# Adding x on GpSimd in SBUF, in place of an identity product on TensorE, for eight output row blocks of a fused attention and gMLP kernel

## The chip, the cores and the metric

One core of a Trainium2 chip runs the kernel. The metric is the device time of one execution in microseconds (us). The kernel before took 169.01 us as the median of three runs (168.78 to 170.12). The execution that was profiled took 168.79 us, of which 167.0 us are the span of the profile. Differences under 1% are not told from no change here.

## The reference

Windowed attention with four sink tokens feeds a gMLP block with spatial gating. All inputs are f32; B = 4, H = 8, S = 768, D = 64, the model width H·D is 512, and d_ff is 1024.

```python
# attention
keep = is_sink | in_window                  # sink: pos < 4; window: 0 <= rel < 128
scores = np.where(keep, q @ k.T / sqrt(D), -1e9)
a = softmax(scores)
x = (a @ v), heads side by side             # (B, S, 512)
# gMLP
h = gelu_tanh(x @ w_in)                     # (B, S, 1024)
u, v = h[..., :512], h[..., 512:]
v_n = (v - mean(v)) / sqrt(var(v) + 1e-6) * g_ln
v_s = einsum('ts,bsd->btd', w_sg, v_n) + b_sg[None, :, None]
out = x + (u * v_s) @ w_out
```

The last line is what the change touches: the sum of the projection and x.

## The kernel before

A batch element is called a block here; there are four, numbered 0 to 3 in the code and first to last in the text. Each has four head pairs, so 16 pairs `n` run through the attention: casts to bf16 on GpSimd (L104, L107), transposes, scores on TensorE (`sc`, L264), exponentials on ScalarE (`ex`, L277), masks on VectorE (L286) or GpSimd (L294, L296), products with v on TensorE (`av`, L320, L326), and the division on VectorE (L328, L329), which leaves x in SBUF as bf16 (`x_sb`, three buffers, one for each block in work).

With the four pairs of a block done, `hidden` runs its first gMLP part: products with w_in (`hv`, `hu`), Gelu on ScalarE, statistics (`st`, L372), an inverse root by nine small VectorE steps (L393 to L402), and six normalising steps (`vn`, L408). The second part of a block is cut into units that wait in a list, `fillers`: eight spatial units (six products `vs`, L418, and then on VectorE `gv`, L421, and `gT`, L424), and six projections, one for each 128 output rows (`project`, a group of four products `o_ps`, L449). The code takes units from that list with `fill` while the attention of the next block runs; so a block's projections stand among the attention of the block behind it. For the blocks before the last the rows are projected in the order 0, 2, 4, 1, 3, 5. The last two or three of a block (rows 3 and 5 of the second, rows 1, 3 and 5 of the third) are taken at the end of the next block's `hidden`, beside its vn steps. The last block has no attention behind it: its units run at the end, with rows 0, 1 and 2 in between the spatial units and rows 3, 4 and 5 at the close; row 5 is cut in two halves (`project_last`).

x reaches the output in one of two ways. With `by_act` false, VectorE adds x while it takes the sum out of PSUM (L452). With `by_act` true, TensorE adds it as a fifth product with an identity matrix (L455), and ScalarE copies the bank to SBUF (L458). Either way SyncE issues the store (L459). The odd rows of the blocks before the last, and all but row 3 of the last, go by ScalarE.

The order on each engine is the order of the program text (`manual_schedule`); nothing moves an instruction. Four PSUM banks turn in `ps_m`, and six SBUF tiles `o_sb` hold rows on their way out. A check at the end counts good reciprocals (L469 to L480, loaded by every engine at L753) and branches to a general version that does not run here.

Of the kernel before, what the change touches and what calls it, by code (L numbers as in the profile page):

```python
# [18 lines left out]
def kernel(  # L19
# [14 lines left out]
    nc = tc.nc  # L34
    V, G, A = nc.vector, nc.gpsimd, nc.scalar
# [7 lines left out]
    NT = S // 128  # L43
    HP = H // 2
    KD = DM // 128
    KU = DF // 128
    NP = B * HP
    HT = NT // 2
# [52 lines left out]
    def cast(n, which, eng):  # L101
        src = raw.pop((n, which))
        if which == "v":
            eng.tensor_copy(v_bufs[n % NV][:, :, :, 0:64], src)  # L104
            return
        dst = work.tile([128, NT, 128], BF16, name=which + "_bf")
        eng.tensor_copy(dst.rearrange("p t (h d) -> p h t d", h=2), src)  # L107
        flat[n, which] = dst

    def load_all(n):  # L110

        for which, m in (("k", n), ("q", n), ("v", n - 1)):
            if m < NP:
                load(m, which, in_rows=m >= FIRST)

    def cast_all(n, parts="kqv"):
        for which in parts:
            m = n - 1 if which == "v" else n
            if m < NP:
                cast(m, which, G)  # L120
# [27 lines left out]
    for i in range(WARM):  # L148
# [3 lines left out]
        out=halves[:, :, 0, :], in_=halves[:, :, 0, :], compare_op=ALU.is_ge, fill=DARK,  # L152
        base=0, pattern=[[0, 2], [1, 128]], channel_multiplier=-1)
    G.affine_select(
        out=halves[:, :, 1, :], in_=halves[:, :, 1, :], compare_op=ALU.is_ge, fill=DARK,
# [53 lines left out]
    def bank(shape, dtype, name):  # L209
        return ps_m.tile(shape, dtype, name=name, tag="m")  # L210

    kTs, qTs, exps, avs = {}, {}, {}, {}
    x_sb, xT = {}, {}
# [85 lines left out]
    def begin_x(b):  # L299
        x_sb[b] = work.tile([128, HP, NT, 128], BF16, name="x", bufs=3)  # L300
        xT[b] = work.tile([128, HP, S], BF16, name="xT")
# [139 lines left out]
                A.copy(o_sb, o_ps[:, 0:m])  # L441
            (nc.sync if eng is V else A).dma_start(out=out[b, rows, cols], in_=o_sb)

    def project(b, t, by_act):
        rows = slice(128 * t, 128 * (t + 1))
        o_ps = bank([128, 512], F32, "o_ps")
        o_sb = small.tile([128, DM], F32, name="o_sb", bufs=6)
        for c in range(KU):
            nc.tensor.matmul(o_ps, gTs[b][:, c, rows], w_out_sb[:, c, :],  # L449
                             start=(c == 0), stop=(c == KU - 1 and not by_act))  # L450
        if not by_act:
            V.tensor_add(o_sb.rearrange("p (h d) -> p h d", h=HP),  # L452
                         o_ps.rearrange("p (h d) -> p h d", h=HP), x_sb[b][:, :, t, :])
        else:
            nc.tensor.matmul(o_ps.rearrange("p (h d) -> p h d", h=HP), iden, x_sb[b][:, :, t, :],  # L455
                             start=False, stop=True)
        if by_act:
            A.copy(o_sb, o_ps)  # L458
        nc.sync.dma_start(out=out[b, rows, :], in_=o_sb)  # L459


    LEAST, MOST = 1e-20, 1e20
# [20 lines left out]
    def general():  # L483
        W = 256 + n_sink
        wide = work.tile([128, 3, W], F32, name="wide", tag="ex", bufs=3)
        V.memset(wide, 1.0)
        m = [wide[:, i, :] for i in range(3)]
        for i in range(3):
            G.affine_select(out=m[i][:, 0:128], in_=m[i][:, 0:128], compare_op=ALU.is_gt,
                            fill=0.0, base=0, pattern=[[1, 128]], channel_multiplier=-1)  # L490
            G.affine_select(out=m[i][:, 128:256], in_=m[i][:, 128:256], compare_op=ALU.is_ge,
                            fill=0.0, base=0, pattern=[[-1, 128]], channel_multiplier=1)
        V.memset(m[0][:, 0:128], 0.0)
        V.memset(m[0][:, 128:128 + n_sink], 0.0)
        V.memset(m[1][:, 0:n_sink], 0.0)
        low = work.tile([128, 3, W], F32, name="low", tag="ex", bufs=3)
        V.tensor_scalar(out=low, in0=wide, scalar1=-1.0, scalar2=1e9,
                        op0=ALU.add, op1=ALU.mult)
        for b in range(B):
            begin_x(b)  # L500
            for hp in range(HP):
                n = HP * b + hp
                for which in "kqv":
                    load(n, which)
                for which in "kqv":
                    cast(n, which, V)
                columns(n, "k", A)
                columns(n, "q", V)
                for i in range(NT):
                    for l in range(2):  # L510
                        stable(n, i, l, m[min(i, 2)], low[:, min(i, 2), :])
                turn_x(n, V)
            hidden(b, {})
            fill(len(fillers))

    def stable(n, i, l, keep, low):
        b, hp = divmod(n, HP)
# [36 lines left out]


    fillers = []

    def fill(count=1):
        for _ in range(count):
            if fillers:  # L560
                fillers.pop(0)()

    def hidden(b, between):
        units = [lambda j=j: hidden_v(b, j) for j in range(NT)]
        units += [lambda f=f, n=n: hidden_u(b, f, n) for n in range(2) for f in range(KU)]
        after = {NT + 1: [lambda: inverse_root(b)]}
        for j in range(NT):
            after.setdefault(NT + 1 + j, []).append(lambda j=j: normalise(b, j))
        for i, unit in enumerate(units):
            unit()  # L570
            for step in after.get(i, []) + between.get(i, []):
                step()
        gate = [[lambda f=f, n=n: spatial(b, f, n) for f in range(KU)] for n in range(2)]
        if b < B - 1:
            fillers.extend(gate[0] + gate[1])
            fillers.extend(lambda t=t: project(b, t, t % 2 == 1) for t in (0, 2, 4, 1, 3, 5))
            return

        rows = [lambda t=t: project(b, t, t != HT) for t in range(NT - 1)]
        fillers.extend(gate[0] + [gate[1][0], rows[0], gate[1][1], gate[1][2], rows[1],  # L580
                                  gate[1][3]] + rows[2:])
        fillers.append(lambda: project_last(b, NT - 1))
# [94 lines left out]
    LAST = NT + 2 * KU - 1  # L677
# [6 lines left out]
    for n in range(HP, NP):  # L684
        todo = valued < n - 1
        block = n % HP == 0 and n > HP
        if HP < n <= 2 * HP:
            load_all(n + 3)
        if n not in exps:
            score(n, 0, 1)  # L690
        if n == HP:
            for si in range(3, NT):
                turn_weights(si, V)
        keep_band(n, 0, V)
        keep_band(n, 1, G)
        if n + 2 >= FIRST:
            cast_all(n + 2, "kq")
        if todo:
            values(n - 1, 0)
        fill(2 if n > HP and not todo else 1)  # L700
        if n + 1 < FIRST and not block:
            columns(n + 1, "k", A)
        if n == HP:
            columns(n + 1, "q", V)
            fill()
        score(n, 2)
        keep_band(n, 2, G)
        if todo:
            values(n - 1, 1)
            if x_by_dma(n - 1):  # L710
                turn_x_by_dma(n - 1)
        if FIRST <= n + 2 < NP:
            columns_by_dma(n + 2)
            if n + 4 == FIRST + 2:
                load_all(n + 4)
        if QUOTA[n] > 2 and todo:
            fill()
        if HP < n < FIRST - 1 and not block:
            columns(n + 1, "q", A if todo else V)
        if n + 2 <= NP:  # L720
            cast_all(n + 2, "v" if n + 2 >= FIRST else "kqv")
        if QUOTA[n] > 1:
            fill()
        if block:
            open_v(n // HP - 1, 0)
            open_v(n // HP - 1, 1)
        if todo and not x_by_dma(n - 1):
            turn_x(n - 1, V)
        if block:
            open_v(n // HP - 1, 2)  # L730
        valued = n - 1
        if block:
            hidden(n // HP - 1, {1: [lambda: values(n, 0)], 3: [lambda: values(n, 1)],
                                 5: [lambda: columns(n + 1, "k", A)] if n + 1 < FIRST else [],
                                 6: [lambda m=m: load_all(m) for m in later.get(n, ())],
                                 7: [lambda: columns(n + 1, "q", A)] if n + 1 < FIRST else [],
                                 9: [lambda: turn_x_by_dma(n) if x_by_dma(n) else turn_x(n, V)],
                                 LAST: [lambda: score(n + 1, 0, 1), lambda: fill(2)]})
            valued = n
# [7 lines left out]
    open_v(B - 1, 2)  # L747
    seen = {}
    hidden(B - 1, {2: [lambda: seen.update(c=count_good())],
                   LAST: [lambda: fill(3)]})  # L750
    seen["t"] = total(seen["c"])
    fill(4)
    count = nc.values_load(seen["t"][0:1, 0:1], min_val=0, max_val=128 * NP * NT * 2)  # L753
# [39 lines left out]
```

## Time and profile before

| | |
|---|---|
| median of three runs | 169.01 us |
| profiled execution | 168.79 us |
| its span | 167.0 us |
| mean granted TensorE clock | 0.993 |
| PE busy | 155.6 us (93%), 1558 matmuls |
| DVE busy | 131.8 us (79%) |
| ACT busy | 109.1 us (65%) |
| POOL busy | 78.1 us (47%) |
| identity products for x, L455 | 13, 379 ns each |
| copies of o_ps by ScalarE, L458 | 13, 593 ns each |
| additions by VectorE, L452 | 10, 682 ns each |
| stores of o_sb, L459 | 23, 256 KB each, median 2.3 us to landing |

PE is TensorE, PEld its weight loads, DVE VectorE, ACT ScalarE, POOL GpSimd, SP SyncE. Matmuls are pipelined, so the 379 ns of one are not its price: consecutive identity or projection products start about 0.22 us apart. The shares of busy time are averages over stages with different limits, so the prediction goes by the stage that each edit stands in.

### The profile page before, as it was taken

What the parts mean: (1) busy time and instruction counts of PE and PEld (TensorE: products, weight loads), DVE (VectorE), ACT (ScalarE), POOL (GpSimd) and SP (SyncE); (2) the same over time, 40 slices, a digit from 0 to 9 for tenths busy, and PEclk for the clock granted to TensorE, in tenths of its full rate; (3) what the DMA queues carried; (4) which work ended last, traced back from release to release, by engine and by line L of the source; (5) the groups of instructions that cost most, each with busy time, mean ns of one, the idle gap of its engine ahead of it and who ended that gap; (6) DMA issues with size and microseconds to landing.
All of it is one profiled execution on the core that took longest, in us unless ns stands there. A gap on an engine that the chain in (4) does not pass through costs nothing.

```text
span 167.0 us, 4051 instructions
## 1 busy us (share of the span) xinstructions
PE 155.6 (93%) x1558; PEld 91.1 (55%) x1558; DVE 131.8 (79%) x317; ACT 109.1 (65%) x148; POOL 78.1 (47%) x115
## 2 busy tenths in 40 slices
PE   3979999999999999999999999999999989999960
PEld 3535574666567665565665655554565635545530
DVE  6756874996899986799888994989999939887620
ACT  3198878889977689688887367679754068621130
POOL 6479771105899979400289996001985000000000
PEclk9999999999999999999999999999999999999997
DMA  4999979999999979999903999899931310050343
GB/s 140 329 323 263 205 104 282 213 317 287 283 220 296 279 247 351 295 215 224 205 20 67 132 238 210 190 228 216 177 76 34 130 63 0 0 194 2 122 151 122
DMA packets 60194, 31.09 MB, mean 186 GB/s; under 512 B 48356, under 2 KB 57080, under 8 KB 60168
## 3 DMA queue, kind: packets, MB, share of 16 engines
q1 hardware_dynamic: 56800, 27.47, 68.8%
q0 software_dynamic: 2944, 2.77, 10.3%
q10 hardware_dynamic: 424, 0.53, 0.9%
q8 instruction: 14, 0.23, 0.6%
q14 instruction: 12, 0.10, 0.2%
HBM read 24.81 MB, written 6.29 MB: 186 GB/s over the span
## 4 chain that ended last, share of the span: by engine, by line
PE 70%; DVE 17%; DMA 5%; issue 1%; ACT 1%; SPq 1%; POOL 1%; POOLq 0%; ACTq 0%
PE vs L418 13%; PE o_ps L449 10%; PE hu L380 9%; PE hv L361 8%; PE av L320 7%; PE sc L264 6%; DMA k_sb<-in_k_dram 5%; DVE gT L424 3%; DVE gv L421 3%; PE hv L368 3%; PE xps L337 2%; DVE st L372 2%; PE av L326 2%; PE qps L219 2%; PE kps L219 2%; DVE vn L408 2%
## 5 line engine op out<-in xcount | busy, mean ns | idle before, releaser
L277 ACT ACTIVATE ex<-sc 128x1024 bf16<-128x1024 f32 x48 | 47.5, 1024 | 12.7 <-PE sc L264 9.2
L418 PE MATMUL vs<-wsgT,vn 128*128 128x384 bf16 x192 | 35.5, 326 | 0.1
L294 POOL TENSOR_SCALAR_AFFINE_SELECT ex<-ex 128x512 bf16<-128x512 bf16 x25 | 17.0, 680 | 30.7 <-issue 15.2
L418 PEld LDWEIGHTS <-vn 128*128 128x128 bf16 x192 | 17.7, 98 | 10.7 <-DVE tot L480 0.4
L449 PE MATMUL o_ps<-w_out_sb,gT 128*128 128x512 bf16 x92 | 23.5, 379 | 0.0
L380 PE MATMUL hu<-xT,w_in_sb 128*128 128x384 bf16 x128 | 22.1, 326 | 0.0
L421 DVE SCALAR_TENSOR_TENSOR gv<-vs,g_sb,b_bc 128x384 bf16<-128x384 f32 x32 | 19.6, 612 | 3.1 <-PE vs L418 2.7
L372 DVE BATCH_NORM_STATS2 st<-v_all 128x6 f32<-128x512 f32 x24 | 16.1, 671 | 5.8 <-ACT v_all L370 5.8
L361 PE MATMUL hv<-w_in_sb,xT 128*128 128x512 bf16 x72 | 18.8, 379 | 0.7 <-ACT v_all L370 0.7
L107 POOL CAST k_bf<-k_sb 128x768 bf16<-128x768 f32 x15 | 13.1, 870 | 13.0 <-DMA k_sb<-in_k_dram 9.0
L329 DVE TENSOR_TENSOR x<-av,rcps 128x384 bf16<-128x384 f32 x32 | 17.8, 557 | 1.1
L424 DVE TENSOR_TENSOR gT<-gv,uT 128x384 bf16<-128x384 bf16 x32 | 17.0, 532 | 1.9
L383 ACT ACTIVATE uT<-hu 128x384 bf16<-128x384 f32 x32 | 15.7, 493 | 4.1 <-PE hu L380 3.7
L458 ACT COPY o_sb<-o_ps 128x512 f32<-128x512 f32 x13 | 7.4, 593 | 14.3 <-PE o_ps L455 12.8
L264 PE MATMUL sc<-qT,kT 64*128 64x256 bf16 x192 | 15.7, 264 | 1.1 <-DVE qT L225 0.7
L380 PEld LDWEIGHTS <-w_in_sb 128*128 128x128 bf16 x128 | 12.3, 98 | 8.0
L370 ACT ACTIVATE v_all<-hv 128x512 f32<-128x512 f32 x24 | 13.1, 600 | 5.0 <-PE hv L368 4.6
L320 PE MATMUL av<-v_sb,ex 128*128 128x65 bf16 x352 | 16.1, 194 | 0.0
L104 POOL CAST v_sb<-v_sb 128x768 bf16<-128x768 f32 x16 | 14.5, 909 | 2.4 <-DMA v_sb<-in_v_dram 2.4
L320 PEld LDWEIGHTS <-ex 128*128 128x128 bf16 x352 | 13.1, 98 | 4.3 <-issue 1.1
L107 POOL CAST q_bf<-q_sb 128x768 bf16<-128x768 f32 x15 | 13.9, 925 | 2.9 <-DMA q_sb<-in_q_dram 2.9
L296 POOL TENSOR_SCALAR_AFFINE_SELECT ex<-ex 128x512 bf16<-128x512 bf16 (+1 forms) x25 | 14.4, 574 | 0.0
(88 smaller groups left out, 218.0 us busy)
## 6 DMA issues: line engine op xcount, KB each, us to landing
k_sb<-in_k_dram SPq DMA_DIRECT2D x16, 384.0 KB, 6.0
v_sb<-in_v_dram SPq DMA_DIRECT2D x16, 384.0 KB, 6.3
out_dram<-o_sb SPq DMA_DIRECT2D x23, 256.0 KB, 2.3
q_sb<-in_q_dram SPq DMA_DIRECT2D x15, 384.0 KB, 5.7
wsg_sb<-in_moe_w_sg_dram POOLq DMA_DIRECT2D x2, 576.0 KB, 10.9
w_in_sb<-in_moe_w_in_dram POOLq DMA_DIRECT2D x2, 256.0 KB, 6.4
w_in_sb<-in_moe_w_in_dram POOLq DMA_DIRECT2D x1, 512.0 KB, 5.4
w_out_sb<-in_moe_w_out_dram POOLq DMA_DIRECT2D x1, 512.0 KB, 9.3
```

What stands on the lines that cost most here:

```text
L107: eng.tensor_copy(dst.rearrange("p t (h d) -> p h t d", h=2), src)
L264: nc.tensor.matmul(sc[:, 512 * l + w:512 * l + w + n_q], kT[rows, 128 * j:128 * (j + 1)], qT[rows, 128 * j:128 * j + n_q], start=not dark, ...
L277: A.activation(out=exps[n][:, g, :], in_=sc, func=AF.Exp, scale=scale)
L320: nc.tensor.matmul(av[:, m, l, :], probs(j, l, half), v_sb[:, l, j, :], start=first, stop=False)
L329: V.tensor_mul(x_sb[b][:, hp, HT * c:HT * (c + 1), :].rearrange("p i (l d) -> p i l d", l=2), av[:, :, :, 0:64], rcp.to_broadcast([128, HT ...
L361: nc.tensor.matmul(hvs[b, j], xT[b][:, c, 128 * j:128 * (j + 1)], w_in_sb[:, c, DF:], start=(c == 0), stop=False)
L372: V.bn_stats(out=st, in_=v_alls[b][:, j, :])
L380: nc.tensor.matmul(h_ps[:, 0:NH], w_in_sb[:, c, 128 * f:128 * (f + 1)], xT[b][:, c, NH * n:NH * (n + 1)], start=(c == 0), stop=(c == KD - 1))
L418: nc.tensor.matmul(vs[:, 0:NH], vns[b][:, si, 128 * f:128 * (f + 1)], wsgT[:, si, cols], start=(si == 0), stop=(si == NT - 1))
L421: V.scalar_tensor_tensor(out=gv, in0=vs[:, 0:NH], scalar=g_sb[:, f:f + 1], in1=b_bc[:, cols], op0=ALU.mult, op1=ALU.add)
L424: V.tensor_mul(gTs[b][:, f, cols], gv, uTs[b][:, f, cols])
L449: nc.tensor.matmul(o_ps, gTs[b][:, c, rows], w_out_sb[:, c, :], start=(c == 0), stop=(c == KU - 1 and not by_act))
```

## The change

Eight of the 13 rows that ScalarE takes out of PSUM lose their identity product: rows 3 and 5 of the second block, rows 1, 3 and 5 of the third, and rows 0, 1 and 2 of the last. For these ScalarE copies the plain sum to `o_sb`, GpSimd adds x to it in place, and then the store is issued. Additions and stores are put off: `project` notes the row in a list, and `add_late` works it off at three places, in the loop over pairs behind the casts, at the end of the last block's `hidden` behind the three projections there, and behind each row of the last block. In GpSimd's queue the second block's two additions come behind the cast of v that follows the masks of pair 13, ahead of the masks of pair 14; the third block's three come before the load of the check's count, the last block's three behind it.

```diff
-    def project(b, t, by_act):
+    late = []
+
+    def project(b, t, by_act, by_pool=False):
...
-                             start=(c == 0), stop=(c == KU - 1 and not by_act))
+                             start=(c == 0), stop=(c == KU - 1 and (by_pool or not by_act)))
+        if by_pool:
+            A.copy(o_sb, o_ps)
+            late.append((b, t, o_sb))
+            return
...
+    def add_late():
+
+        while late:
+            b, t, o_sb = late.pop(0)
+            o = o_sb.rearrange("p (h d) -> p h d", h=HP)
+            G.tensor_add(o, o, x_sb[b][:, :, t, :])
+            nc.sync.dma_start(out=out[b, 128 * t:128 * (t + 1), :], in_=o_sb)
...
+    held = {0: (), 1: (3, 5), 2: (1, 3, 5)}
...
-            fillers.extend(lambda t=t: project(b, t, t % 2 == 1) for t in (0, 2, 4, 1, 3, 5))
+            fillers.extend(lambda t=t: project(b, t, t % 2 == 1, t in held[b]) for t in (0, 2, 4, 1, 3, 5))
...
-        rows = [lambda t=t: project(b, t, t != HT) for t in range(NT - 1)]
+        def row(t):
+            project(b, t, t != HT, t < HT)
+            add_late()
+
+        rows = [lambda t=t: row(t) for t in range(NT - 1)]
...
@@ loop over pairs @@
             cast_all(n + 2, "v" if n + 2 >= FIRST else "kqv")
+        add_late()
...
-                   LAST: [lambda: fill(3)]})
+                   LAST: [lambda: fill(3), add_late]})
```

More of the change, by code (lines that the diff above doesn't have):

```diff
@@ L721 @@
             cast_all(n + 2, "v" if n + 2 >= FIRST else "kqv")
+        add_late()
         if QUOTA[n] > 1:
```

## The prediction

> **What bounds the kernel now.** The chain of waits on the page comes first: shares of the span by engine.
>
> ```profile
> PE 70%; DVE 17%; DMA 5%; issue 1%; ACT 1%; SPq 1%; POOL 1%; POOLq 0%; ACTq 0%
> ```
>
> TensorE carries 70% of the path, so one instruction fewer there seems to pay. But it need not pay where the eight instructions stand, so the chain in order of time is read next, from 110 us on (start, length, piece).
>
> ```profile
> 114.05 0.86 PE o_ps L449 x4
> 114.91 0.22 PE o_ps L455
> 115.13 0.99 PE vs L418 x6
> 116.14 0.63 DVE gv L421
> ...
> 129.02 0.34 PE xps L337 x3
> ...
> 145.24 2.83 DVE vn L408 x6
> ...
> 148.14 4.23 PE vs L418 x25
> ...
> 158.31 0.22 PE o_ps L455
> ```
>
> An identity product (L455) takes 0.22 us of the path. From 116.1 to 129.0 the chain is on VectorE, from 129.0 to 134.8 on TensorE, from 136.8 to 148.1 on VectorE again, and from 148.1 to 161.5 on TensorE. The windows cut at these points (busy time per engine, granted clock, DMA):
>
> ```profile
> 143.00:148.10 5.10, 5.10 (x27) 2.25 (x24) 4.73 (x19) 2.84 (x6) 0.00 (x0) 1.00 0.24 92
> 148.10:161.50 13.40, 13.35 (x77) 7.35 (x76) 8.69 (x19) 2.36 (x5) 0.00 (x0) 1.00 0.26 97
> 161.50:167.00 5.50, 0.00 (x0) 0.00 (x0) 0.00 (x0) 0.36 (x1) 0.00 (x0) 0.80 0.37 126
> ```
>
> In the first, VectorE is full and TensorE's matmuls are fillers; in the second TensorE is full. GpSimd (the fifth figure) is idle in both, which is where six of the eight adds go. Last, the timeline around 117 to 124 us, VectorE, then GpSimd, then the one TensorE group that matters:
>
> ```profile
> 117.77 0.86 DVE L424 TENSOR_TENSOR gT<-gv,uT 128x384 bf16<-128x384 bf16 x1
> 125.43 0.36 DVE L424 TENSOR_TENSOR gT<-gv,uT 128x384 bf16<-128x384 bf16 x1
> 117.60 0.82 POOL L107 CAST k_bf<-k_sb 128x768 bf16<-128x768 f32 x1
> 118.36 0.95 POOL L107 CAST q_bf<-q_sb 128x768 bf16<-128x768 f32 x1
> 120.35 1.27 POOL L104 CAST v_sb<-v_sb 128x768 bf16<-128x768 f32 x1
> 122.16 0.63 POOL L296 TENSOR_SCALAR_AFFINE_SELECT ex<-ex 128x512 bf16<-128x512 bf16 x1
> 124.11 0.36 PEld L320 LDWEIGHTS <-ex 128*128 128x128 bf16 x10 [0.21 <-issue]
> ```
>
> The gT product takes 0.36 us while GpSimd is idle (125.43). The one that starts at 117.77, during a cast, ends at 118.63, 0.26 after the cast gives way at 118.36, and the next cast takes 0.95 instead of 0.82. The same holds for the others that start inside a GpSimd instruction: they take turns, one whole instruction each. The gv product (one operand in PSUM) takes 0.61 or 0.62 whatever GpSimd does.
>
> **The change part by part.** *Eight identity products go*: 8 x 0.22 = 1.7 us of TensorE, in three places.
> - Two (rows 3 and 5 of the second block, near 114 us): TensorE reaches the vs products 0.43 earlier, but VectorE is busy until 115.97 and waits only 0.17 for them (116.14). Gain at most 0.17, and only if nothing later on this stretch decides.
> - Three (rows 1, 3, 5 of the third block, 143.7 to 147.1): what follows on TensorE waits for the sixth vn, which ends at 148.07. Gain 0.
> - Three (rows 0, 1, 2 of the last block): the chain is TensorE throughout. Gain 3 x 0.22 = 0.65.
>
> *ScalarE* copies the same banks for the same 0.59, and may start 0.22 earlier; the second block's pair stays where it was, behind two exponentials until 115.98. No change.
>
> *Eight adds on GpSimd.* No row shows a GpSimd instruction with two inputs. From below: one input of 512 elements takes 0.63 (L294, L296). From above: two such passes, 1.26. The select over 256 elements takes 0.42, so 256 more elements cost about 0.22; a second stream of 512 adds 0.44 to 0.63, which gives 1.07. I take 1.1, nearest to the row with its second operand read in turn; started back to back, instructions overlap by 0.05 (0.63 long, 0.59 apart), so 1.05 each. The Trainium skill (GPSIMD Engine Reference, § 3.1) gives 4497 ns for an add over 2048 elements, which by proportion is an estimate of 1.12, and its § 4.1 says not to put a two-input add on this engine.
>
> *Second block's two adds, behind the value cast of 120.35.* On GpSimd's queue they stand in front of the masks of the next head pair. The cast gives way at 121.57, and that pair's first mask group now ends at 122.79 (122.16 + 0.63). It will be late by 2 x 1.05, and by two gT products that now fall ahead of it (0.24 each): 2.6, so 125.4. The value products that read it started at 124.11: TensorE waits 1.3. It is dense from there to the transposes at 129.02, before which it stood idle for 0.28; so the path is 1.0 later at 129.02, and from there TensorE carries it on. VectorE's own chain would be some 0.5 later (one mask product and a gT that meet GpSimd), which lies inside that 1.0; so does the 0.17 gained. With adds of 0.63 the wait is 0.3 and is absorbed: 0. With 1.26 it is 1.6: 1.3 later. SyncE issues the two stores behind the adds, and the x transpose queued behind them (issued at 123.73) goes out about 1 us later; its reader is the hv product at 131.9, so some 7 us cover it.
>
> *Third block's three adds.* The copies end near 145.4, 146.3 and 147.1, and VectorE begins its six vn at 145.24, on the path. A vn over 512 f32 elements of SBUF is busy for 0.54 (0.47 from one to the next), the statistics over the same operand (L372) for 0.67: vn reads at a faster pace. Does it share GpSimd's port as gT does? The nearest row is a mask step of the same operation (L165, one SBUF input, 8.05 to 8.33): the cast that GpSimd started at 8.13 took 0.88 instead of 0.82, so it was held as behind a gT. I take it that vn and adds take turns. Each add then costs the vn chain its 1.05 less the 0.12 of a vn's start-up that overlaps (gT: 0.24 after its wait against 0.36 alone): 0.93, and 2.8 for three. With 0.63 it is 1.4, with 1.26 it is 3.3; if vn needs no turn, 0. The Trainium skill (GPSIMD Engine Reference, § 1) has the two engines contend where VectorE runs a 2-port mode or has two SBUF inputs. For the second half the gT rows agree; for the first only the 0.06 of the mask step speaks here. By that rule the sum is the one I take; without its first half it is the first rival. GpSimd's and SyncE's loads of the check count come after these adds; nobody waits for them before the end.
>
> *Last block's three adds.* A gT that meets an add waits: the second, by about 0.1 to 0.3, the fourth by 0.4. Row 3's last product needs that fourth gT and has 0.4 of slack: 0. The third add ends some 1.2 after its copy, 0.7 before the store of row 4 can go; so no store on SyncE's queue is held up. Were an add to take 1.9, the last stores would be late.
>
> *The sum*: +1.0 + 2.8 - 0.65 = +3.15 against the profiled execution, 168.79 us (span 167.0 and 1.8 around it). That is 171.9; the median of the runs is 0.2 higher than the profiled one, so 172.0.
>
> **The rivals.**
> - *The vn steps pass beside the adds* (not slower). They have one SBUF input, as gv and the x product have, and these never grow under GpSimd. Against it: the faster pace and the mask step's 0.06. The third block's 2.8 goes, and the time is 168.79 + 1.0 - 0.65 = 169.1. It decides if GpSimd's adds end about 1.1 after each copy while vn still ends 2.83 after it begins.
> - *VectorE keeps the port through its six vn*, since one vn starts before the one ahead has ended (0.54 long, 0.47 apart). Then the adds run from 148.1 beside the gate products. Three gT wait for one add each; by the fourth, VectorE is about 0.4 behind and row 0's last product, which already waits 0.2 for it, is as late: 169.5. For gT and the mask product back to back (119.30, 120.11) GpSimd got its turn between them, which speaks against it.
> - *Short adds*, 0.63: 0 + 1.4 - 0.65, and 0.17 gained: 169.4.
> - *TensorE's clock falls in the hole.* With vn late, TensorE has five or six lone matmuls between 146.7 and 151. In the last window the granted clock averages 0.80 over 5.5 us, so it went to one half about 3.3 us after the last matmul. A hole of 4 us with little in it can do that. If return takes as long as the fall, 3.3 us at half pace lose 1.7: 173.6. For: the length; against: the lone matmuls inside. The Trainium skill (TensorE: Matmul & The Clock Gate, Part 1) puts the fall behind an idle window of about 3.4 us; the 3.3 measured here agrees.
> - *All eight products count and the adds cost nothing*: 167.1. The 0.17 at 116.14 and the vn chain speak against it.
>
> **How the numbers follow.** A difference under 1% (1.7 us) can't be told from no change here. Forecast, 172.0 (its own range 171.0 to 172.7): 0.45. Vn beside the adds, 169.1: 0.17. Port kept by VectorE, 169.5: 0.15. Short adds, 169.4: 0.08. Clock, 173.6: 0.12. All gains free, 167.1: 0.03. Slower by over 1% (above 170.7) is the first and the clock: 0.57. The three between are the same: 0.40. Faster: 0.03. The range from 168.5 to 173.0 leaves out the clock and the free gains, 0.15, and a little of the forecast's upper tail.
>
> **What would show it.** Right: the two adds near 122 at about 1.1 us each; the value products of the pair behind at about 125.4 with a wait on GpSimd's mask; six vn that span 5 to 6 us with adds between them; TensorE dense from there to the end, 0.65 shorter. Wrong: vn still 2.83 long beside adds, adds that start only after the last vn, or adds near 0.6. A granted clock under 1.0 behind the vn stretch is the clock's case.

## The result, and the profile after

The changed kernel took 173.78 us (median of six runs, 172.95 to 174.84) against 168.84 for the kernel before: a ratio of 1.0291, 95% interval 1.0261 to 1.0322. The profiled execution took 174.84, with a span of 173.1, and is the slowest of the six. In three of the six the mean granted clock was 0.974 to 0.977 and the time 174.4 to 174.8; in the other three it was 0.985 to 0.994 and the time about 173.0.

On the chain of waits TensorE's share falls from 70% to 65%, and VectorE's rises from 17% to 19%. The chain ends with the last copy, so the longer end behind it (7.9 us, below) is not in these shares.

```profile
PE 65%; DVE 19%; DMA 3%; SPq 3%; ACT 2%; issue 2%; POOL 1%; ACTq 0%; POOLq 0%
```

The chain in order of time, after (start, length, piece):

```profile
129.45 0.34 PE xps L337 x3
...
145.67 4.89 DVE vn L408 x5
...
150.61 6.12 PE vs L418 x26
156.73 0.86 PE o_ps L451 x4
...
161.38 2.59 PE o_ps L451 x12
163.97 0.22 PE o_ps L461
...
165.20 0.37 ACT o_last L441
```

Five vn take 4.89 us where six took 2.83. Behind them 26 vs products take 6.12, 0.24 each, where 25 took 4.23, 0.17 each. The three rows 2, 3 and 4 follow in one piece of 2.59 with no identity product of row 2 between them. The last copy starts at 165.20, and the span ends 7.9 us behind it; before, it was 161.49 and 5.5.

The windows, cut at the end of vn, at the last copy and at the end of the span:

```profile
145.60:151.10 5.50, 3.15 (x13) 1.00 (x12) 5.43 (x8) 1.35 (x3) 3.95 (x3) 0.95 0.33 126
151.10:165.20 14.10, 14.07 (x74) 7.51 (x73) 8.75 (x18) 2.34 (x4) 3.46 (x3) 0.90 0.15 54
165.20:173.10 7.90, 0.00 (x0) 0.00 (x0) 0.00 (x0) 0.37 (x1) 0.00 (x0) 0.66 0.38 129
```

GpSimd, idle here before, is busy for 3.95 us in the first, and TensorE for only 3.15 of 5.5. The granted clock is 0.95 and then 0.90. At half pace for the missing share, that is 2 x 0.05 x 5.5 + 2 x 0.10 x 14.1 = 3.4 us at half clock. A narrower window shows where:

```profile
150.60:154.00 3.40, 3.39 (x11) 1.53 (x12) 1.92 (x5) 0.00 (x0) 0.00 (x0) 0.50 0.24 84
```

The timeline puts the adds and the vn side by side (vn on VectorE, adds on GpSimd):

```profile
145.67 5.33 DVE L408 TENSOR_SCALAR vn<-v_all,mv,y 128x512 bf16<-128x512 f32 x6
145.86 3.95 POOL L472 TENSOR_TENSOR o_sb<-o_sb,x 128x512 f32<-128x512 f32 x3 [16.30 <-ACT o_sb L454]
```

The listing of vn by tile (shortest, median and longest, in ns) gives the length of a vn that had to wait:

```profile
L408 DVE TENSOR_SCALAR vn<-v_all,mv,y x24: 534/542/1377, 35.2 to 150.5; 128x512 bf16<-128x512 f32 x24
```

One table sums both profiled executions (us from the start of the span):

| milestone | before | after | gained (-) or lost in the stage |
|---|---|---|---|
| score products ahead of the second block's last rows | 112.32 | 112.12 | -0.20, ahead of the change |
| transposes behind the second block's adds | 129.02 | 129.45 | +0.63 |
| first vn of the last block | 145.24 | 145.67 | 0 |
| last vn ends | 148.07 | 151.00 | +2.50 |
| row 0's products start | 152.36 | 156.73 | +1.44 |
| last copy starts | 161.49 | 165.20 | -0.66 |
| end of the span | 167.0 | 173.1 | +2.4 |

No case of the prediction had a price for the last row. SyncE's issues of stores at the end, before and then after:

```profile
160.20 1.82 SPq L459 DMA_DIRECT2D out_dram<-o_sb  x2
162.12 0.52 SPq L442 DMA_DIRECT2D out_dram<-o_last  x1
```

```profile
164.12 0.33 SPq L473 DMA_DIRECT2D out_dram<-o_sb  x1
164.55 1.87 SPq L465 DMA_DIRECT2D out_dram<-o_sb  x2
166.51 0.41 SPq L442 DMA_DIRECT2D out_dram<-o_last  x1
```

And what SyncE then waited for at the final branch (total, times, longest), before and after:

```profile
SPq L757 <- SPq L757: 2.0, 1, 2.0
```

```profile
SPq L778 <- SPq L778: 3.9, 1, 3.9
```

Before, the last store left 0.63 us after the last copy started; after, 1.31. The store of row 2 leaves at 164.12, when its add is done, and that of row 3 right behind it at 164.55, though VectorE had finished row 3 at 163.89. The last store then lands 4.3 us after its issue; before, the ScalarE half of the same row, the one whose landing the profile has, took 2.8.

In three of the profiled executions below the granted clock also stands at one half for about 3.4 us near 13 us (a 5 in the fourth of the page's 40 slices), ahead of every change, and what follows comes 1.1 to 1.3 us later; there, stages are compared and not totals. The ratios leave out executions more than 1.5% above the fastest of their kernel; the medians keep them.

### The profile page after: what moved, and what is told of

Its sections match the earlier page's. It is cut to its first block, busy times and chain, and to the rows that moved or that the text cites. A ratio compares the mean times of both kernels' runs of the same rounds, so it can differ in the third digit from the quotient of the medians.

```text
span 173.1 us, 4054 instructions
## 1 busy us (share of the span) xinstructions
PE 156.0 (90%) x1550; PEld 90.8 (52%) x1550; DVE 135.6 (78%) x317; ACT 109.1 (63%) x148; POOL 88.3 (51%) x123
## 4 chain that ended last, share of the span: by engine, by line
PE 65%; DVE 19%; DMA 3%; SPq 3%; ACT 2%; issue 2%; POOL 1%; ACTq 0%; POOLq 0%
PE vs L418 13%; PE hu L380 9%; PE o_ps L451 8%; PE hv L361 8%; PE av L320 6%; PE sc L264 5%; DMA q_sb<-in_q_dram 3%; DVE gT L424 3%; DVE vn L408 3%; PE hv L368 3%; SPq L95 3%; DVE gv L421 3%; DVE x L329 2%; PE xps L337 2%; DVE st L372 2%; DVE ex L286 2%
## 5 line engine op out<-in xcount | busy, mean ns | idle before, releaser
L418 PE MATMUL vs<-wsgT,vn 128*128 128x384 bf16 x192 | 37.8, 337 | 2.4 <-DVE vn L408 2.2
L294 POOL TENSOR_SCALAR_AFFINE_SELECT ex<-ex 128x512 bf16<-128x512 bf16 x25 | 17.1, 685 | 28.8 <-ACT ex L277 13.5
L418 PEld LDWEIGHTS <-vn 128*128 128x128 bf16 x192 | 18.2, 100 | 14.9 <-DVE vn L408 3.6
L472 POOL TENSOR_TENSOR o_sb<-o_sb,x 128x512 f32<-128x512 f32 x8 | 9.8, 1237 | 27.1 <-ACT o_sb L454 18.6
L451 PE MATMUL o_ps<-w_out_sb,gT 128*128 128x512 bf16 x92 | 22.8, 379 | 0.2 <-DVE x L329 0.2
L107 POOL CAST k_bf<-k_sb 128x768 bf16<-128x768 f32 x15 | 12.5, 836 | 13.0 <-PE sc L264 6.9
L424 DVE TENSOR_TENSOR gT<-gv,uT 128x384 bf16<-128x384 bf16 x32 | 17.7, 553 | 1.9
```

The lines of the kernel that those rows point to most:

```text
L418: nc.tensor.matmul(vs[:, 0:NH], vns[b][:, si, 128 * f:128 * (f + 1)], wsgT[:, si, cols], start=(si == 0), stop=(si == NT - 1))
L424: V.tensor_mul(gTs[b][:, f, cols], gv, uTs[b][:, f, cols])
```

## The experiments

**Each place alone.** The table `held` and, for the last block, the last argument in `row` say which rows keep GpSimd's adds; the first two edits:

```diff
-    held = {0: (), 1: (3, 5), 2: (1, 3, 5)}
+    held = {0: (), 1: (3, 5), 2: ()}        # second block alone
+    held = {0: (), 1: (), 2: (1, 3, 5)}     # third block alone
-            project(b, t, t != HT, t < HT)
+            project(b, t, t != HT)          # in both
```

> Only rows 3 and 5 of the second block keep GpSimd's adds; all other rows are as before. As forecast, the masks that wait behind the two adds hold TensorE and the path is 1.0 us longer: 169.8. As the changed kernel's trace reads (transposes at 129.45 against 129.02, and everything ahead 0.2 earlier), VectorE's chain is 0.6 longer: 169.4. If the two identity products count and the adds are hidden: 168.4.

Measured: 169.81 against 168.91, ratio 1.0054 (1.0016 to 1.0092). From the score products (112.07) to the transposes (129.39) the profiled execution took 17.32 us, before 16.70: 0.62 longer. The median is the forecast's number, but its interval spans 0.3 to 1.6 us and can't tell 0.6 from 1.0; the stage can, and it did not go by the forecast's route. First TensorE's timeline, then the chain:

```profile
124.30 0.30 PE L320 MATMUL av<-v_sb,ex 128*128 128x65 bf16 x4 [0.41 <-POOL ex L294]
```

```profile
121.51 1.14 DVE gT L424
...
125.75 0.82 DVE ex L286
...
127.83 0.81 DVE gT L424
...
129.39 0.34 PE xps L337 x3
```

TensorE waited 0.41 for GpSimd's mask, not 1.3: only the first of the two mask instructions (L294) held these products, and of the two gT that I put ahead of it one came later. The chain does not pass there. It runs through VectorE without a break from 119.5, where gT and mask products take turns with GpSimd.

> Only rows 1, 3 and 5 of the third block keep GpSimd's adds. If vn and adds take turns, three vn take about 1.4 us each, the six span 5.3 instead of 2.8, and the time is 2.5 longer, 171.3; if the clock also falls in TensorE's hole, 1.7 more, 173.0. If vn passes beside the adds and the delay came from elsewhere: 168.8.

Measured: 173.76 against 168.91, ratio 1.0291 (1.0275 to 1.0307), as long as the whole change. The six vn spanned 145.96 to 151.30, 5.34 us. The window behind them, to the last copy, shows the clock:

```profile
151.30:166.40 15.10, 15.00 (x76) 7.94 (x76) 8.86 (x19) 2.35 (x5) 0.00 (x0) 0.89 0.20 74
```

From the last vn to the last copy it is 15.09 us against 13.42 before, with the same instructions: 1.67 for a clock of 0.89. What this execution has over the 173.0 expected lies elsewhere: its score products near 113 were 0.71 late already, ahead of its edit, and its end is 6.0 us instead of 5.5.

```diff
-    held = {0: (), 1: (3, 5), 2: (1, 3, 5)}
+    held = {0: (), 1: (), 2: ()}            # last block alone
```

> Only rows 0, 1 and 2 of the last block keep GpSimd's adds. As forecast, TensorE's close is 0.65 us shorter and nothing else moves: 168.2. If the stores of the last rows are held behind the third add on SyncE's queue, as the changed kernel's end suggests (its last store is issued 1.4 us after its data against 0.8 before), the gain shrinks to nothing: 168.8 or a little more.

Measured: 170.49 against 168.91, ratio 1.0118 (1.0087 to 1.0149). Both expectations were too low. From the last vn (147.83) to the last copy (160.60) it took 12.77, which is 0.65 less than before, as forecast; but the span ended 8.2 us behind that copy instead of 5.5. SyncE's stores, and its last wait:

```profile
159.51 0.33 SPq L473 DMA_DIRECT2D out_dram<-o_sb  x1
159.94 1.88 SPq L465 DMA_DIRECT2D out_dram<-o_sb  x2
161.91 0.41 SPq L442 DMA_DIRECT2D out_dram<-o_last  x1
```

```profile
SPq L778 <- SPq L778: 3.8, 1, 3.8
```

**The third block's adds behind the last vn.**

```diff
+    def behind_vn():
+        peek = small.tile([128, 1], BF16, name="peek", bufs=1)
+        G.tensor_copy(peek, vns[B - 1][:, NT - 1, 0:1])
...
-                   LAST: [lambda: fill(3), add_late]})
+                   LAST: [lambda: fill(3), behind_vn, add_late]})
```

> The whole change, but a one-column copy of the last vn on GpSimd stands ahead of the third block's three adds, so that they start when vn is done. If vn and adds take turns, vn spans 2.8 again, TensorE has no hole, its clock stays at 1.0, and the adds cost the gT products at most 0.4: about 170 instead of 173.8. If the delay isn't the adds' (the copies' or the products' new order, say), the time stays near 173.8.

Measured: 171.35 against 168.91, ratio 1.0175 (1.015 to 1.0201), and 2.4 less than the whole change. The windows of vn and of what follows:

```profile
145.90:148.80 2.90, 2.61 (x12) 0.87 (x10) 2.88 (x7) 1.32 (x3) 0.00 (x0) 1.00 0.00 0
148.80:163.50 14.70, 13.05 (x73) 6.89 (x73) 11.60 (x19) 2.35 (x5) 7.22 (x7) 1.00 0.33 122
```

With GpSimd idle the six vn again take 2.83, and the clock stays at 1.0: the adds were what held vn. But they don't run free behind it. VectorE is busy for 11.60 us instead of 8.69 before, six gT products wait for adds (up to 1.34 us each), and the stage takes 14.74 where the run with the last block's adds alone took 12.77. So three adds beside the gate products, with the delays that they bring on, cost 2.0 and not the 0.4 that I expected. In this run the last four stores of SyncE leave 0.9 to 1.5 us apart (160.76, 162.21, 163.16, 164.09), and the span ends 5.8 us behind the last copy with all three late adds in place.

**Spare products in TensorE's hole**, 14 of them (`keep_busy`), the whole change otherwise:

```diff
-                   LAST: [lambda: fill(3), add_late]})
+                   LAST: [lambda: fill(3), add_late, lambda: keep_busy(14)]})
```

> The whole change, and 14 spare products (0.22 us each, into a bank that nobody reads) on TensorE behind the third block's last row, where it waits for vn. They add work. If the clock's fall in the hole is what lengthened the products behind it (26 of them in 6.1 us instead of 4.3), the clock stays at 1.0, vn still spans 5.3, and the time is 1.7 shorter than the change's: 172.1. If the hole isn't the cause: 173.8 or more.

Measured: 173.16 against 169.09 (ratio 1.0204, 1.0146 to 1.0261). The six runs scatter from 172.0 to 174.83, and three of the six of the change itself lie near 173.0, so the medians do not show the 1.7. The profiled executions do, one of each: 173.08 against 174.84 for the change, 1.76 less with 14 products more. The windows of vn and of what follows:

```profile
145.60:151.00 5.40, 5.29 (x26) 2.22 (x24) 5.39 (x7) 1.30 (x3) 3.95 (x3) 1.00 0.33 124
151.00:163.70 12.70, 12.62 (x72) 7.06 (x73) 8.68 (x19) 2.35 (x4) 3.47 (x3) 1.00 0.17 61
```

TensorE is busy through vn, the clock stays at 1.0, and from the last vn (150.95) to the last copy (163.72) it takes 12.77, as in the run with the last block alone. The vn still span 5.34. The mean clocks of all executions fit, a weaker sign since other falls lower them too: with the hole left as it is, three of six of the change and all five of the third block alone are at 0.974 to 0.980; with the spare products none of six is under 0.981. So the hole let the clock fall, if not in every execution, and vn's turns made the hole.

**Which store lengthens the end.** First without row 2's add:

```diff
-    held = {0: (), 1: (3, 5), 2: (1, 3, 5)}
+    held = {0: (), 1: (), 2: ()}
...
-            project(b, t, t != HT, t < HT)
+            project(b, t, t != HT, t < HT - 1)
```

> Only rows 0 and 1 of the last block keep GpSimd's adds; row 2 has its identity product again. TensorE's close is 0.43 us shorter than before. If the longer end of the run with three rows (8.2 us from the last copy to the end of the span, against 5.5) comes from the store of row 2, which leaves at the same moment as that of row 3, the end is 5.5 again and the time 168.5. If any late add in the last block lengthens the end: about 170.5.

Measured: 168.9 against 169.09, ratio 0.9988 (0.995 to 1.0026). The end behind the last copy is 5.9 us, near the kernel before. The 0.43 that TensorE saves nearly goes into the 0.4 by which the end is still longer.

Then all three rows, with row 2's store on ScalarE's queue (`add_late` is cut into `add`, the addition, and `store`, which issues the store from a given engine; `held` names no row, as above):

```diff
         def row(t):
             project(b, t, t != HT, t < HT)
-            add_late()
+            if t < HT - 1:
+                add_late()
+            elif t == HT - 1:
+                add(*late[0])                       # the add alone
+            elif t == NT - 2:
+                store(*late.pop(0), A)              # row 2's store, behind the copy of row 4
```

> Only rows 0, 1 and 2 of the last block keep GpSimd's adds, and the store of row 2 is issued by ScalarE behind its copy of row 4, so that SyncE's stores of rows 3, 4 and 5 no longer stand behind it. If the crowding of SyncE's stores lengthens the end: 168.2, with 5.5 us behind the last copy. If the end is longer for another reason: 170.5, as with three rows.

Measured: 169.8 against 169.09, ratio 0.9998 (0.9958 to 1.0039). The profiled execution has the early fall of the clock; its end is 6.2 us behind the last copy, 2.0 less than with the same three adds and all stores on SyncE. Row 2's store still leaves 0.37 us from row 3's (161.03 and 160.66), but on the other queue. SyncE's last wait:

```profile
SPq L788 <- SPq L788: 2.2, 1, 2.2
```

Then the crowding alone, in the kernel before, without any add on GpSimd:

```diff
-        nc.sync.dma_start(out=out[b, rows, :], in_=o_sb)
+        crowd.append((out[b, rows, :], o_sb))
+        if (b, t) != (B - 1, HT - 1):               # row 2 waits for row 3
+            while crowd:
+                o, i = crowd.pop()
+                nc.sync.dma_start(out=o, in_=i)
...
+    crowd = []
```

> The kernel before, with no add on GpSimd; only the store of row 2 of the last block is issued behind that of row 3 on SyncE's queue, so that the last four stores of SyncE leave close together. If crowded stores alone lengthen the end, as with GpSimd's three adds (8.2 us behind the last copy), it is 7 to 8 us here too, and the time is 170.5 to 171. If the longer end needs GpSimd's late adds (their own end, or GpSimd's late branch): 5.5 us and 168.9.

Measured: 172.24 against 169.79, ratio 1.0156 (1.0104 to 1.0207). SyncE's stores and its last wait:

```profile
161.44 2.41 SPq L463 DMA_DIRECT2D out_dram<-o_sb  x3
163.94 0.43 SPq L442 DMA_DIRECT2D out_dram<-o_last  x1
```

```profile
SPq L762 <- SPq L762: 3.8, 1, 3.8
```

The last copy starts at 162.72 and the span ends at 170.5: 7.8 us, as expected of the crowding, with GpSimd idle. The total is above the 170.5 to 171 expected; the profiled execution has the early fall of the clock. Row stores that crowd on SyncE's queue in the last 3 us before the final one cost some 2 us here, whoever computed the rows.

Last, the three rows' stores issued by GpSimd itself (`add(*late[0])`, then `store(*late.pop(0), G)`; `held` names no row):

> Only rows 0, 1 and 2 of the last block keep GpSimd's adds, and GpSimd issues their stores itself, so that SyncE has only rows 3, 4 and half of row 5 at the end. TensorE's close is 0.65 us shorter. If crowding on SyncE's queue is the cause: an end of 5.5 us and 168.2, faster than the kernel before. If stores leaving together crowd the transfers themselves, or GpSimd's issue is slow: 169 to 170.5.

Measured: 169.79 against 169.79, ratio 1.0023 (0.9986 to 1.0061). TensorE's stage is 12.77 again, and the end 6.1 us: neither 5.5 nor 8. The 0.65 saved on TensorE is given back at the end.

**The second block's adds one pair later**, where GpSimd had stood idle:

```diff
-    held = {0: (), 1: (3, 5), 2: (1, 3, 5)}
+    held = {0: (), 1: (3, 5), 2: ()}
...
-            project(b, t, t != HT, t < HT)
+            project(b, t, t != HT)
...
-        add_late()
+        if n % HP == 2:
+            add_late()
```

> As in the run with the second block's two adds alone, but they stand one pair later in GpSimd's queue, behind the next cast of v, where GpSimd stood idle for 1.5 us. If TensorE's wait for the masks behind the adds is the cost (forecast): it is gone, 168.7. If VectorE's turns with GpSimd are the cost: its gT and mask products of 125 to 126 us meet the adds instead, and the time stays between 169.3 and 169.8.

Measured: 170.23 against 169.09, ratio 1.0011 (0.9971 to 1.0051). The profiled execution has the early fall of the clock, so the stage is compared: 113.66 to 130.43, 16.77 us, 0.07 over the kernel before. GpSimd and VectorE there, and then the same mask product before:

```profile
126.03 2.84 POOL L472 TENSOR_TENSOR o_sb<-o_sb,x 128x512 f32<-128x512 f32 x2
```

```profile
126.22 1.64 DVE L286 TENSOR_TENSOR ex<-ex,mask 128x1024 bf16<-128x1024 bf16 x1
```

```profile
125.70 0.69 DVE L286 TENSOR_TENSOR ex<-ex,mask 128x1024 bf16<-128x1024 bf16 x1
```

The mask product still waits for an add and takes 1.64 us instead of 0.69, but the gT of this stage meet less of GpSimd's work: the last four ahead of the transposes take 0.36 to 0.60, where they took 0.55 to 1.14 with the adds one pair earlier. Neither expectation in its plain form holds: the loss went without TensorE's mask wait having been its cause, and VectorE's turns depend on which of its products meet an add.

No version here is faster than the kernel before by more than its interval.

## Why the prediction was wrong

- **The step that failed** is the last block's: "so no store on SyncE's queue is held up". The third add did end 0.8 us before the store of row 4 could go, as I worked out. But the store that matters is row 3's: its data were ready at 163.89, it stood behind row 2's store, which waited for the add until 164.12, and it left at 164.55. I priced a held store at nothing and looked for the danger in an add of 1.9 us. The crowded stores cost 2.4 in the profiled execution, 0.7 of it in the later issue of the last store; that crowding alone does this was shown without GpSimd.
- **The clock** was a rival with 0.12, priced at 1.7. It came in the profiled execution (1.44) and in the third block's run (1.67), and the spare products took it away. The pattern of the six runs, three near 173.0 and three near 174.6, fits a fall in some and not in others; only one of them has a trace. The argument against it, the lone matmuls in the hole, did not hold: four lone products and the first of the next run, begun between 146.8 and 150.2, did not keep the clock up. The Trainium skill (TensorE: Matmul & The Clock Gate, Part 1) speaks of an idle window of about 3.4 us; a window with some work in it was enough here.
- **Vn and adds taking turns** was right: three vn of 1.37 us, +2.5 against 2.8 forecast, gone when the adds wait for vn. The rivals "the vn steps pass beside the adds" and "VectorE keeps the port" fall. What each add costs was set 0.1 too high: 0.83, not 0.93. The Trainium skill's rule (GPSIMD Engine Reference, § 1, a 2-port mode on VectorE) agrees with these 1.37 us; that vn runs in such a mode stands in no row of the profile, only its pace points to it.
- **The add's length**, taken as 1.1, is 1.15 where nothing is in its way, so "short adds" falls too. The estimate of 1.12 from the Trainium skill (GPSIMD Engine Reference, § 3.1) agrees.
- **The second block** was mis-routed and mis-sized: +0.63 for +1.0. TensorE's wait for the mask was 0.41 and off the path; what I called "some 0.5 later ... inside that 1.0" was the path itself.
- **TensorE's saving in the last block**, 0.65, was right to 0.01, and worth nothing at the end.

Forecast terms +1.0 + 2.8 - 0.65 came out as +0.63 + 2.50 - 0.66. That alone, on 168.79 and less the 0.2 by which this execution was early ahead of the change, would have been 171.1; the end's 2.4 and the clock's 1.4 took it out of the range. Without the clock's term these numbers give 173.5, and the three shorter executions took 173.0, still above the forecast's own 171.0 to 172.7: the end's term alone was enough to miss that.

Open: why crowded stores land late. The profile shows SyncE's longer issue (1.2 us for row 3's store) and the longer landing. The packets in the traces say where most of the landing's delay lies. Each store here lands in 16 parts. In the changed kernel 15 parts of the last store had landed by 169.40; the packets of the sixteenth began at 169.60, when a 16 KB packet of the program's own instructions (queue q8 of the page, 168.67 to 169.62) had ended, and it landed at 170.85. The three other runs with a long end (the last block alone, the spare products, the crowding alone) have such a part too, which begins within 0.02 us of the end of such a packet and lands 0.7 to 1.5 us behind the other fifteen; the runs with a short end have none. That is seen in the traces and not tested: no run moved the instruction packet, and how the crowding brings the last store behind it stays open.

## What to carry to other kernels

Work moved to an idle engine isn't free when the two engines take turns at memory: before moving an add, list which instructions of the neighbour on the path would meet it, and price each meeting at the mover's whole length. A stall that leaves TensorE nearly idle can also cost what it does to TensorE's clock, 1.4 to 1.7 us here. And the last stores of a kernel are a path of their own: work out when each becomes ready against the one queued in front of it.

## What the runs showed of the hardware

A VectorE instruction with one SBUF input (vn, f32 to bf16) waits for a running GpSimd instruction just as those with two do, 1.37 us against 0.54, while one with an operand in PSUM (gv) stays at 0.60 to 0.62 beside adds. Two 256 KB stores issued 0.4 us apart on one queue near the end made the last store land 4.3 us after its issue (4.2 to 4.5 in the three other runs that had such a pair). With few products in a stretch of 4 us, TensorE's granted clock stood at 0.50 for 3.4 us.
